# Keys of the last 768 tokens by seven block products, and second channel weights converted later

## The chip, the cores and the metric

The kernel runs on one core of a Trainium2 chip. The metric is the device time of one execution in microseconds; the median of three runs of the kernel before is 672.54 (672.38 to 672.57). TensorE does the matrix products, VectorE (DVE) and ScalarE (ACT) the elementwise work, GpSimd (POOL) some memsets, and SyncE (SP) issues every DMA.

## The reference

Three layers follow each other: windowed attention over 4 batches of 576 tokens and 8 heads of 64, a channel-mixing layer, and a mixer over tokens and channels. Cut to what the change touches:

```python
xk = mu_k * x + (1.0 - mu_k) * x_prev        # x: (4, 576, 512)
k = np.maximum(xk @ w_k, 0.0)                # w_k: (512, 1024)
v = k * k @ w_v                              # w_v: (1024, 512)
r = 1.0 / (1.0 + np.exp(-(xr @ w_r)))
x = r * v
...
h = np.maximum(xt @ w_tok1, 0.0) @ w_tok2    # over tokens
u = x + h.transpose(0, 2, 1)
h2 = np.maximum(u @ w_ch1, 0.0) @ w_ch2      # w_ch1: (512, 1536), w_ch2: (1536, 512)
return u + h2
```

## The kernel before

Every 32-bit product is made of three matmuls (`mm3`): operands are split into a high and a low half (`split`: a copy that rounds, on ScalarE or VectorE, and a subtraction on VectorE), and high x high, high x low and low x high are summed in a PSUM bank.

The stages in order of time. Attention of batch 0 runs first, beside the loading and conversion of `w_k`, `w_v`, `w_r`. Then a loop over `g` = 0 to 49 walks six chunks of 384 tokens (`c, m = divmod(g, 8)`): `prep` mixes each token with the one ahead of it and splits it, `keys(c, m)` makes 128 of the 1024 key columns for the chunk in one bank (4 blocks of 128 input channels, so 12 matmuls), squares and splits them, `mix` multiplies them with `w_v`, `receptance` does `w_r`. The table `beside` spreads the 27 attention units of batches 1 to 3 over the loop, 9 to a chunk pair. Then follow the token stage (`tokens_in`, `tokens_out`), the channel stage's first pass (`middle(c, j)`, 3 chunks of 768 tokens by 6 blocks of 256 hidden columns, results stored in `part_mid`), and its second pass (`result(c)`).

The token stage and both channel passes use seven block products in place of eight (a Strassen form, names A11, S1, A12, S2, S4, S3, A22): sums of quarters of the weights and of the inputs are made first, and the products are accumulated in banks x, y and z. In `middle`, S2, S3 and A22 go on in the bank of A11, S4 in that of S1; between them the bank is copied out (`aside`) or added to others (`part`).

The quarters of the channel weights have to be converted from the stored 64-bit form, combined, split, and stored in DRAM drawers (`part_w0` to `part_w5` for the first weights, `part_A11`, `part_S1` and so on for the second), from which they are fetched later. `weight_1` runs at `g` in `W1_AT`, `weight_2` three times at `g` in `W2_AT`, and three times after the blocks `W2_LATE` = 4, 8, 12 of `middle`. `slowly` lets the planner put such work up to 20 us later than it is written. One conversion of second weights is two loads of 512 KB, 2 x 3 operations to decode, 4 sums, 7 splits and 7 stores of 256 KB. The fetches of all seven products' second weights stand behind `middle` in the program; their places (`w2_at`) are those of the first weights, which the last chunk's blocks set free one after the other, and, for two thirds into A12, a place that the conversions use for their results (slot x2, number 4).

A planner (`Plan.order`) fixes the order of instructions on each engine ahead of the run, with costs of its own and due times counted back from TensorE's order. Each engine then works through its list in order; a DMA on SP that waits holds up the ones behind it. All the work is recorded at one line of the file (L412), so the tile names tell operations apart.

## Time and profile before

| what | value |
|---|---|
| median of three runs | 672.54 us |
| the profiled execution | 672.25 us, span 670.5 us |
| TensorE busy | 657.9 us, 98% of the span, 4129 matmuls |
| VectorE, ScalarE busy | 542.0 and 363.6 us |
| DMA | 138.05 MB, mean 206 GB/s |

Stages on the clock of the span: attention of batch 0 and the start of chunk 0 up to about 69 us, chunks 0 to 3 with attention up to 257, chunks 4 and 5 up to 345, the token stage up to 402, the channel stage's first pass up to 533, its second pass to the end. The profile's first table gives the busy time of each engine; views by stage follow below. A matmul's duration overlaps with the next one's, so that the time of many in a row is read from the pitch of a row without gaps.

### The profile page before, as it was taken

How to read it: one execution, taken by the hardware profiler on the slowest of the kernel's cores; microseconds unless marked ns; L12 is line 12 of the kernel's file. 1: busy time of each engine (PE TensorE's matmuls, PEld its weight loads, DVE VectorE, ACT ScalarE, POOL GpSimd, SP SyncE). 2: the span in 40 equal slices, each digit the busy share in tenths (PEclk: the TensorE clock that was granted, in tenths of full speed). 3: DMA queues.
4: the chain of work that ended last, by engine and by line, in shares of the span. 5: the costliest groups of instructions: out<-in, count | busy, mean ns of one | idle time of the engine just before them, and what ended most of it. 6: DMA issues, size and time to landing. Idle time of an engine off the chain costs nothing.

```text
span 670.5 us, 11406 instructions
## 1 busy us (share of the span) xinstructions
PE 657.9 (98%) x4129; PEld 608.2 (91%) x4129; DVE 542.0 (81%) x1143; ACT 363.6 (54%) x944; POOL 2.3 (0%) x22
## 2 busy tenths in 40 slices
PE   6999999999999999999999999999999999999997
PEld 6778888899898898888889899999999999999997
DVE  3999997799589589588789779698698659899982
ACT  4989775678567568476656346174284222312310
POOL 0000000000000000000000000000000000000000
PEclk9999999999999999999999999999999999999999
DMA  8989343557637243527952118849688999933211
GB/s 316 386 319 320 118 144 99 179 151 233 188 123 240 84 139 119 172 107 271 304 201 62 66 50 288 326 154 322 231 294 281 358 411 412 390 117 94 71 37 59
DMA packets 60776, 138.05 MB, mean 206 GB/s; under 512 B 5296, under 2 KB 23856, under 8 KB 59696
## 3 DMA queue, kind: packets, MB, share of 16 engines
q1 hardware_dynamic: 60720, 137.33, 58.7%
q8 instruction: 32, 0.52, 0.3%
q14 instruction: 24, 0.20, 0.1%
HBM read 91.70 MB, written 45.61 MB: 205 GB/s over the span
## 4 chain that ended last, share of the span: by engine, by line
PE 82%; DMA 10%; DVE 5%; ACT 2%; issue 1%; SPq 0%; DVEq 0%; ACTq 0%
PE bank L412 82%; DMA x<-w_k 2%; DMA z<-part_mid 2%; DMA outT<-y 1%; DMA at<-part_mid 1%; ACT x L412 1%; DVE z L412 1%; DMA wr<-units 1%; DVE wv L412 1%; DMA wv<-units 1%; DVE x L412 1%; DMA raw<-w_v 1%; DVE at L412 1%; DVE xt L412 1%; ACT xt L412 0%
## 5 line engine op out<-in xcount | busy, mean ns | idle before, releaser
L412 PE MATMUL bank<-z,wk 128*128 128x384 f32 x800 | 176.1, 343 | 0.8 <-DVE z L412 0.5
L412 PEld LDWEIGHTS bank<-z,wk 128*128 128x128 f32 x800 | 140.6, 188 | 8.0 <-ACT z L412 1.3
L412 PE MATMUL bank<-wv,z 128*128 128x512 f32 x432 | 126.1, 403 | 0.0
L412 PEld LDWEIGHTS bank<-wv,z 128*128 128x128 f32 x432 | 77.8, 188 | 12.7
L412 ACT ACTIVATE at<-at 128x96 f32<-128x96 f32 (+2 forms) x178 | 64.6, 365 | 35.4 <-DVE at L412 34.1
L412 DVE TENSOR_TENSOR z<-z,z 128x384 fp32r<-128x384 f32 (+1 forms) x94 | 52.9, 570 | 18.7 <-ACT z L412 17.2
L412 PE MATMUL bank<-wr,z 128*128 128x512 f32 x228 | 62.5, 402 | 1.0 <-DVE z L412 1.0
L412 ACT ACTIVATE z<-z 128x384 fp32r<-128x384 f32 (+1 forms) x112 | 57.6, 523 | 6.9 <-DVE z L412 4.0
L412 PE MATMUL bank<-xt,wk 128*128 128x384 f32 x254 | 54.0, 346 | 0.2
L412 PEld LDWEIGHTS bank<-wr,z 128*128 128x128 f32 x228 | 41.4, 188 | 8.5 <-DVE z L412 1.3
L412 PE MATMUL bank<-xt,x 128*128 128x384 f32 x248 | 48.6, 334 | 0.0
L412 PE MATMUL bank<-z,x 128*128 128x384 f32 x232 | 47.1, 335 | 0.3 <-DVE at L412 0.3
L412 PEld LDWEIGHTS bank<-xt,wk 128*128 128x128 f32 x254 | 44.4, 188 | 1.8 <-issue 0.5
L412 DVE TENSOR_TENSOR at<-bank,at 128x384 f32<-128x384 f32 x64 | 35.2, 551 | 12.4 <-PE bank L412 11.9
L412 ACT ACTIVATE z<-bank 128x384 f32<-128x384 f32 (+1 forms) x52 | 25.0, 484 | 35.7 <-PE bank L412 35.5
L412 PEld LDWEIGHTS bank<-xt,x 128*128 128x128 f32 x248 | 43.5, 188 | 0.0
L412 PEld LDWEIGHTS bank<-z,x 128*128 128x128 f32 x232 | 40.7, 188 | 0.7 <-DVE at L412 0.6
L412 DVE SCALAR_TENSOR_TENSOR z<-xt,cst,z 128x256 f32<-128x256 f32 (+3 forms) x92 | 34.1, 402 | 0.2
L412 ACT ACTIVATE x<-bank 96x512 f32<-96x512 f32 (+1 forms) x45 | 26.3, 589 | 10.2 <-PE bank L412 9.9
L412 ACT ACTIVATE at<-bank 128x384 f32<-128x384 f32 x33 | 15.9, 488 | 27.1 <-PE bank L412 26.4
L412 ACT ACTIVATE z<-xt,cst 128x256 f32<-128x256 f32 (+3 forms) x65 | 25.9, 433 | 6.5 <-DVE z L412 6.1
L412 DVE TENSOR_TENSOR raw<-raw 128x256 f32<-128x256 f32 (+1 forms) x68 | 27.7, 421 | 0.9 <-ACT raw L412 0.6
(190 smaller groups left out, 1191.3 us busy)
## 6 DMA issues: line engine op xcount, KB each, us to landing
part_mid<-at SPq DMA_DIRECT2D x18, 768.0 KB, 4.6
z<-part_mid SPq DMA_DIRECT2D x11, 576.0 KB, 8.7
x<-w_c SPq DMA_DIRECT2D x12, 512.0 KB, 4.5
at<-units SPq DMA_DIRECT2D x14, 416.0 KB, 4.7
unit<-units SPq DMA_DIRECT2D x13, 416.0 KB, 4.8
at<-units SPq DMA_DIRECT2D x21, 256.0 KB, 3.8
part_w<-wv SPq DMA_DIRECT2D x21, 256.0 KB, 3.2
part_w<-x SPq DMA_DIRECT2D x21, 256.0 KB, 4.0
```

The lines of the kernel that those rows point to most:

```text
L412: call(kw["out"], kw["constant"]) if method == "memset" else call(**kw)
```

## The change

The keys of chunks 4 and 5 (the last 768 tokens) are made together, by seven block products. New functions: `weight_ks` makes the four sums of quarters of `w_k` for a pair of key blocks j and j + 4, splits and stores them (`part_k0` to `part_k3`), at `g` in `K_AT` = 9, 12, 16, 19; `fetch_k` loads them; `pair_keys(j)` makes the products for blocks j and j + 4 and both chunks. The loop runs over four chunks only, and the code behind it makes keys, `mixes` and `receptance` of chunks 4 and 5. `prep`'s elementwise part becomes `shift`. All six `weight_2` stand after the blocks 4, 6, 8, 10, 12, 14 of `middle`; the first weights are converted at other `g`, and the attention units end at 58 half steps, where they ended at 68. The tracking of DRAM drawers becomes finer (by 384 columns, in `_cells`). Cut to its core:

```diff
-W1_AT, W2_AT, W2_LATE, SLACK = range(10, 34, 4), range(35, 47, 4), (4, 8, 12), 20.0
+W1_AT, K_AT, W2_LATE, SLACK = (8, 11, 13, 16, 18, 21), (9, 12, 16, 19), (4, 6, 8, 10, 12, 14), 20.0
...
-    for n, (lo, hi) in enumerate(([0, 20], [20, 42], [42, 68])):
+    for n, (lo, hi) in enumerate(([0, 20], [20, 40], [40, 58])):
...
+    def weight_ks(j):
+
+        full, sums = at(("raw", 0, 0), (2, 4, 128)), at(("raw", 0, 1024), (4, 2, 128))
+        for i in range(2):
+            combine(full[:, i], *(f(w) for w in wk[j + 4 * i]), ALU.add)
+        (a11, a12), (a21, a22) = ((full[:, i, :2], full[:, i, 2:]) for i in range(2))
+        combine(sums[:, 0], a21, a22, ALU.add)
+        combine(sums[:, 1], sums[:, 0], a11, ALU.subtract)
+        combine(sums[:, 2], a11, a21, ALU.subtract)
+        combine(sums[:, 3], a12, sums[:, 1], ALU.subtract)
+        for n, i in enumerate((0, 1, 3, 2)):
+            t = fresh.tile(2, 2, 128, dtype=F32R)
+            split(sums[:, i], t[:, 0], t[:, 1])
+            nc.sync.dma_start(out=kept_k[j][:, n], in_=f(t.flat(2)))
...
-    nchunk = len(CHUNKS)
+    nchunk = len(CHUNKS) - 2
...
-        if g in W2_AT:
-            slowly(weight_2, W2_AT.index(g), early)
+        if g in K_AT:
+            slowly(weight_ks, K_AT.index(g))
...
+    split(b11, *xk["A11"])
+    combine(d1, b12, b11, ALU.subtract)
+    split(d1, *xk["S1"])
+    split(b21, *xk["A12"])
+    combine(d2, b22, d1, ALU.subtract)
+    split(d2, *xk["S2"])
+    split(b22, *xk["S4"])
+    combine(d1, b22, b12, ALU.subtract)
+    split(d1, *xk["S3"])
+    combine(d2, b21, d2, ALU.subtract)
+    split(d2, *xk["A22"])
...
+    x_r, y_r, z_r, k_ring = psum(0, 3), psum(1, 4), psum(2), psum(3, 4, 0, 1, 2)
...
+    def pair_keys(j, w):
+        x, y, z = (r.tile(N2) for r in (x_r, y_r, z_r))
...
+        on = dict(first=False, goes_on=True)
+        by(x, "A11")
+        s1 = aside(x)
+        by(y, "S1")
+        s5 = aside(y)
+        by(z, "A12")
+        part(k2[4, j], z, s1)
+        by(x, "S2", **on)
+        s2 = aside(x)
+        by(y, "S4", **on)
+        part(k2[5, j], y, s2)
+        by(x, "S3", **on)
+        part(k2[5, j + 4], x, s5)
+        by(x, "A22", **on)
+        relu(k2[4, j + 4], x)
+        square(k2[4, j + 4])
...
+    ws = {j: fetch_k(j) for j in range(2)}
+    for j in range(4):
+        pair_keys(j, ws[j])
+        if j < 2:
+            ws[j + 2] = fetch_k(j + 2)
+        for n in (2 * j - 1, 2 * j):
+            if 0 <= n < 6:
+                mixes(4, n)
...
             if 6 * c + j in W2_LATE:
-                slowly(weight_2, len(W2_AT) + W2_LATE.index(6 * c + j), late)
+                slowly(weight_2, W2_LATE.index(6 * c + j), late)
```

How the order of instructions moves is shown at three places. In the names, the first number is left out where several slots share a name, and the last counts tiles; `part_S_78` is the drawer of S1, `part_A_77` that of A11, `part_A_79` that of A12, `part_S_82` that of S3, `part_A_83` that of A22, and `part_mid_87` holds the first pass's results of chunk 0.

SP before, around the end of the channel stage's first pass (the last two stores of the last conversion come first):

```order
L412 DMA part_A_83<-x_1_4319 128x512
L412 DMA part_S_82<-at_1_2580 128x512
L412 DMA raw_0_316<-part_u_84 128x768
L412 DMA part_mid_89<-at_2_4110 512x1x384
L412 DMA wk_0_370<-part_A_77 128x2048
L412 DMA wk_0_598<-part_A_77 128x1024
L412 DMA part_mid_89<-at_2_4110 512x1x384
L412 DMA wk_0_598<-part_S_78 128x1024
L412 DMA wk_0_711<-part_S_78 128x2048
L412 DMA z_1_5146<-part_mid_87 128x1152
L412 DMA wk_1_778<-part_A_79 128x2048
L412 DMA x_1_4319<-part_A_79 128x1024
```

And SP now, at the same place, from the last conversion's first store (A11) on:

```order
L421 DMA part_A_77<-at_1_3192 128x512
L421 DMA wk_1_782<-part_A_79 128x2048
L421 DMA z_1_5244<-part_mid_87 128x1152
L421 DMA wk_0_602<-part_A_77 128x1024
L421 DMA part_A_79<-x_1_4313 128x512
L421 DMA part_S_78<-x_1_4313 128x512
L421 DMA part_mid_89<-at_2_4116 512x1x384
L421 DMA z_3_5294<-part_mid_87 128x1152
L421 DMA wk_0_715<-part_S_78 128x2048
L421 DMA z_3_5316<-part_mid_87 128x1152
L421 DMA part_S_80<-y_3_4329 128x512
L421 DMA raw_2_3334<-part_mid_87 128x1152
```

The stores of the last conversion, which stood ahead of all fetches, now stand between them; those of S3, A22 and S4 follow further down, and the fetch of A12's last part (into x_1_4313) behind them.

TensorE now, in the new stage for the keys of the last two chunks (bank_63 and bank_66 are the two x banks, bank_64 a y bank):

```order
L421 MATMUL bank_63<-z_0_475,wv_1_597 128x384 x6
L421 MATMUL bank_66<-unit_1_2782,wk_0_715 128x384
L421 MATMUL bank_66<-unit_1_2805,wk_0_715 128x384
L421 MATMUL bank_66<-unit_1_2782,wk_0_715 128x384 x2
L421 MATMUL bank_66<-unit_1_2805,wk_0_715 128x384
L421 MATMUL bank_63<-x_1_2762,raw_1_2895 128x384
L421 MATMUL bank_63<-x_1_1229,raw_1_2895 128x384
```

The first row is S2 of a pair, the last two are the beginning of its S3; between them stand five matmuls of another pair's A22. These rows are new; before, every key block was one group of 12 matmuls in a bank of its own.

VectorE now, at the end of the channel stage's first pass (bank_68, bank_70 and bank_65 hold S1, A12 and the x sum of the very last block; x_1 rows are low halves of the last conversion):

```order
L421 TENSOR_TENSOR x_1_4313<-raw_2_3334,x_1_4313 128x256
L421 COPY at_2_4067<-bank_68 128x384
L421 TENSOR_TENSOR x_1_4313<-raw_2_3334,x_1_4313 128x256
L421 TENSOR_TENSOR at_2_4116<-bank_70,at_2_4067 128x384
L421 TENSOR_SCALAR at_2_4116<-at_2_4116 128x384
L421 TENSOR_TENSOR at_2_4116<-bank_65,at_2_4067 128x384
L421 TENSOR_SCALAR at_2_4116<-at_2_4116 128x384
L421 TENSOR_TENSOR y_3_4329<-raw_2_3334,y_3_4329 128x256
L421 TENSOR_TENSOR at_2_4116<-bank_68,wr_2_4092 128x384
L421 TENSOR_TENSOR at_1_3192<-raw_2_3334,at_1_3192 128x256
L421 TENSOR_TENSOR wv_2_3601<-z_1_5244,wv_2_3601 128x1152
L421 CAST x_1_4313<-raw_2_3334 128x256
```

```order
L421 TENSOR_TENSOR x_1_4313<-raw_2_3334,x_1_4313 128x256
L421 TENSOR_TENSOR wv_2_3601<-z_3_5294,wv_2_3601 128x1152
L421 TENSOR_TENSOR x_1_4313<-raw_2_3334,x_1_4313 128x256
```

The second piece follows directly on the first: the low halves of A22 and S3 around a subtraction that takes a load from `part_mid_87`. Before, VectorE's queue has none of the conversion's operations here.

## Rows read from the trace of the kernel before

**Rows 1.** The page: busy us of each engine, share of the span, instructions.

```profile
PE 657.9 (98%) x4129; PEld 608.2 (91%) x4129; DVE 542.0 (81%) x1143; ACT 363.6 (54%) x944; POOL 2.3 (0%) x22
```

**Rows 2.** Busy us by stage: stretch, length, engines, clock, DMA share, GB/s.

```profile
0.00:69.00 69.00, 60.71 (x472) 50.21 (x473) 57.33 (x126) 55.50 (x174) 1.08 (x20) 1.00 0.90 328
69.00:257.00 188.00, 188.00 (x1348) 167.05 (x1348) 153.75 (x403) 131.35 (x421) 0.00 (x0) 1.00 0.48 152
257.00:345.00 88.00, 88.00 (x442) 77.32 (x441) 68.01 (x178) 54.96 (x128) 1.18 (x2) 1.00 0.65 219
...
402.00:533.00 131.00, 130.71 (x752) 129.72 (x752) 106.91 (x196) 61.27 (x122) 0.00 (x0) 1.00 0.78 281
533.00:670.50 137.50, 133.51 (x767) 132.44 (x765) 108.60 (x117) 29.69 (x28) 0.00 (x0) 1.00 0.54 202
...
68.00:97.00 29.00, 28.50 (x242) 25.08 (x241) 28.68 (x65) 22.71 (x73) 0.00 (x0) 1.00 0.42 121
```

**Rows 3.** What TensorE waited for: us in total, times, longest.

```profile
PE bank L412 <- DMA at<-cst: 4.9, 1, 4.9
...
PE bank L412 <- DVE at L412: 0.9, 3, 0.5
```

**Rows 4.** Timeline of TensorE, 505 to 580 us: start, us, instructions, idle before.

```profile
524.27 4.32 PE L412 MATMUL bank<-z,x 128*128 128x384 f32 x24
...
534.59 1.33 PE L412 MATMUL bank<-z,x 128*128 128x384 f32 x6 [0.28 <-DVE at L412]
...
541.49 7.96 PE L412 MATMUL bank<-xt,wk 128*128 128x384 f32 x45
```

**Rows 5.** Groups by form: count, busy us, mean ns, idle before and its cause.

```profile
L412 DVE TENSOR_TENSOR x<-raw,x 128x256 fp32r<-128x256 f32 x32 | 13.4, 420 | 0.3
...
L412 DVE SCALAR_TENSOR_TENSOR raw<-x,raw 128x512 uint16<-128x512 uint32 x12 | 9.0, 748 | 0.1
...
L412 DVE TENSOR_TENSOR unit<-wv,unit 128x768 f32<-128x768 f32 x6 | 5.7, 950 | 0.0
...
L412 DVE TENSOR_TENSOR wv<-z,wv 128x1152 f32<-128x1152 f32 x5 | 6.8, 1351 | 0.3 <-DMA z<-part_mid 0.3
...
L412 DVE TENSOR_TENSOR at<-bank,at 128x384 f32<-128x384 f32 x64 | 35.2, 551 | 12.4 <-PE bank L412 11.9
L412 ACT ACTIVATE z<-bank 128x384 f32<-128x384 f32 (+1 forms) x52 | 25.0, 484 | 35.7 <-PE bank L412 35.5
```

**Rows 6.** Issues on SP: start, us, instructions.

```profile
522.58 1.57 SPq L412 DMA_DIRECT2D wk<-part_S  x2
```

**Rows 7.** DMA, 505 to 545 us: KB each, median us to landing.

```profile
z<-part_mid SPq DMA_DIRECT2D x3, 576.0 KB, 7.7
...
wk<-part_S SPq DMA_DIRECT2D x1, 1024.0 KB, 8.0
x<-part_S SPq DMA_DIRECT2D x1, 1024.0 KB, 12.7
...
x<-part_A SPq DMA_DIRECT2D x1, 512.0 KB, 9.0
...
part_S<-x SPq DMA_DIRECT2D x1, 256.0 KB, 3.6
...
part_S<-at SPq DMA_DIRECT2D x1, 256.0 KB, 6.0
```

**Rows 8.** DMA, 452 to 482 us: KB each, median us to landing.

```profile
wr<-w_c SPq DMA_DIRECT2D x4, 512.0 KB, 5.6
...
part_A<-x SPq DMA_DIRECT2D x2, 256.0 KB, 2.1
```

**Rows 9.** Busy us in two stretches of 5 us, columns as in rows 2.

```profile
545.00:550.00 5.00, 5.00 (x31) 5.00 (x30) 5.00 (x5) 2.78 (x3) 0.00 (x0) 1.00 1.04 420
575.00:580.00 5.00, 4.85 (x28) 4.53 (x28) 4.22 (x5) 1.56 (x2) 0.00 (x0) 1.00 1.03 418
```

**Rows 10.** The chain that ended last: start, us, what.

```profile
527.58 5.11 DMA z<-part_mid
```

More of the change, by code (lines that the diff above doesn't have):

```diff
@@ L194, in _cells @@
         if not isinstance(a, View):
-            return [a.name]
+            if not a.name.startswith("part"):
+                return [a.name]
+            (row, _), *free = a.ap
+            lo = a.offset % row
+            hi = lo + sum((n - 1) * step for step, n in free)
+            return [(a.name, cell) for cell in range(lo // N2, hi // N2 + 1)]
         offset, ((_, parts), *free) = a.pattern
@@ L682, in prep, with shift @@
         tmp = tmp_r.tile(n)
+        shift(tmp, c, which, kt)
+        r = sets[(c + 1 + which) % 2]
+        h, l = (r.tile(n, dtype=F32R) for _ in range(2))
+        split(tmp, h, l)
+        xs[c, which, kt] = (h, l)
+    def shift(tmp, c, which, kt):
+        pieces = CHUNKS[c]
         col = slice(4 * which + kt, 4 * which + kt + 1)
@@ L699, in prep @@
             o += k
-        r = sets[(c + 1 + which) % 2]
-        h, l = (r.tile(n, dtype=F32R) for _ in range(2))
-        split(tmp, h, l)
-        xs[c, which, kt] = (h, l)
     KT = [2, 3, 0, 1]
@@ L823, in tile_model @@
             k_ring, s_ring = psum(3, 4), psum(0)
-        if 2 * g > [42, 68][1] and s_ring:
-            k_ring, s_ring = psum(3, 4, 0, 1, 2), None
         if m == 0 and c < nchunk:
@@ L852, in tile_model, with product, relu @@
             attend(h, s_ring, t_ring, x_ring)
+    def product(out, a, b, first=True, last=True, goes_on=False):
+        for k, ((ah, al), (bh, bl)) in enumerate(zip(a, b)):
+            mm3(out, ah, al, bh, bl, first and k == 0, last and k == len(b) - 1, goes_on)
+    def relu(out, in_):
+        nc.either(
+            ("scalar", "activation", dict(out=out, in_=in_, func=AF.Relu)),
+            ("vector", "tensor_scalar", dict(out=out, in0=in_, scalar1=0.0, scalar2=None, op0=ALU.max)),
+        )
@@ new lines, in pair_keys, with by, aside, part @@
+    def pair_keys(j, w):
+        x, y, z = (r.tile(N2) for r in (x_r, y_r, z_r))
+        k2[4, j], k2[4, j + 4] = lo_r.tile(N2), lo_r.tile(N2)
+        k2[5, j], k2[5, j + 4] = hi_r.tile(N2), hi_r.tile(N2)
+        def by(out, name, **kw):
+            a, b = ([tuple(v[:, k] for v in hl) for k in range(2)] for hl in (w[name], xk[name]))
+            product(out, a, b, **kw)
+        def aside(p):
+            t = aside_r.tile(N2)
+            copy(t, p)
+            return t
+        def part(t, p, more):
+            combine(t, p, more, ALU.add)
+            relu(t, t)
+            square(t)
+        on = dict(first=False, goes_on=True)
[14 more added lines that the diff above has]
+        square(k2[4, j + 4])
@@ new lines, in tile_model, with mixes @@
+    order_m = [0, 4, 1, 5, 2, 6, 3, 7]
+    def mixes(c, n, first=5):
+        m = order_m[n]
+        h, l = (k2_r.tile(N2, dtype=F32R) for _ in range(2))
+        split(k2[c, m], h, l)
+        for j in range(TILES[c]):
+            if n == 0:
+                vp[j] = bank(first + j, (C,))
+            mm3(vp[j], h[:, rows(j)], l[:, rows(j)], *wv[m], n == 0, n == 7)
+            if n == 7:
+                t = x2[FIRST[c] + j]
+                nc.vector.scalar_tensor_tensor(out=t, in0=t, scalar=1.0, in1=vp[j], op0=ALU.add, op1=ALU.mult)
@@ L1019, in tile_model @@
     tokens_out(B - 1)
-    def product(out, a, b, first=True, last=True, goes_on=False):
-        for k, ((ah, al), (bh, bl)) in enumerate(zip(a, b)):
-            mm3(out, ah, al, bh, bl, first and k == 0, last and k == len(b) - 1, goes_on)
     for j in range(3, 6):
```

61 lines of the change are left out of this document (53 added, 8 removed).

## The prediction

> **What bounds the kernel now.** I read the share of each engine first [rows 1]: TensorE is busy 657.9 us, 98% of the span. Then the busy time by stage [rows 2]: before 69 us TensorE has 8.3 us of gaps (it waits there for inputs and for VectorE), from 69 to 345 us it has none, in the channel stage's first pass 0.29 us, and 4.0 us behind 533 us, nearly all of it the tail after the last matmul. The longest wait of TensorE, 4.9 us, is at the very start [rows 3]. So between 69 and 667 us the time is the number of matmuls by their pitch, and an edit is worth the matmuls that it saves, less the waits that it opens. The pitch of a 128x384 matmul is read from an unbroken row [rows 4]: 24 in 4.32 us; the last one's 0.33 us overlaps nothing behind it, so (4.32 - 0.33) / 23 = 0.1735 us.
>
> The profiled execution took 672.25 us (span 670.5, and 1.75 around it); the median of the runs shown is 672.54, 0.29 above. I sum against 672.25 and add the 0.29 at the end.
>
> **The keys' products.** Before, two chunks of 384 tokens need 2 x 8 x 4 x 3 = 192 matmuls for their keys; now 4 pairs x 7 products x 2 x 3 = 168. Nothing else on TensorE changes in number. 24 x 0.1735 = 4.2 us saved, all of it on the path, since TensorE has no gap there [rows 2].
>
> **What stands beside it.** The seven products need sums of weights (four calls) and of inputs. A call has on VectorE 2 sums of 512 columns, at most 0.75 each, and 8 operations of 256 columns at 0.42 [rows 5], so 4.9; its four copies can go to ScalarE. Four calls add 20 us to VectorE in the stretch 69 to 257 us, where it is busy 153.8 of 188 [rows 2]; 174 of 188 leaves 14, and two attention units that come earlier take part of that. The stretch 68 to 97 us shows VectorE busy 28.68 of 29 with TensorE at 28.50 [rows 2], so such a load is survivable. If this cover were gone, each 1% too much would cost 1.9 us. I take 0.3, between 0 and 2.
>
> In the pairs' own stage VectorE was busy 68 of 88 us [rows 2]. Three conversions of second channel weights leave it, some 7 us each: 11 operations of 256 columns at 0.42, two of 512 at 0.75 [rows 5], and two cheaper ones. About 14 come: five sums and three more low halves of 768 columns at 0.95 and 12 additions at 0.55 [rows 5]. So VectorE hides them. But the order is tight. A product that goes on in a bank has to wait until the bank has been read (TensorE's excerpt shows S2 in bank_63, five other matmuls, then S3 in the same bank: 5 x 0.1735 = 0.87 us for a copy of 0.48 on ScalarE or an addition of 0.55 on VectorE [rows 5], and two hand-overs). I count eight such places in the order, where by these durations the reading operation ends less than 0.1 us ahead of the matmul. Each costs between nothing and 0.5 us, the longest single wait of TensorE for such an addition; the mean there was 0.3 (0.9 in 3) [rows 3]. I take 1.5 for all, between 0 and 4.
>
> **The conversions moved into the channel stage's first pass.** Three of six move from the stage 257 to 345 us into 402 to 533 us. Each loads 2 x 512 KB and stores 7 x 256 KB, 2.8 MB, so 8.5 MB more in 131 us: 65 GB/s on top of 281 [rows 2]; the queue ran at 420 where it was full [rows 9]. VectorE's 3 x 7 = 21 us come on top of 106.9 of 131 [rows 2]: 128 at most, less what ScalarE, with 61.3, takes over of other work. On average both fit, VectorE barely: each 1% too much would cost 1.3 us here. I take nothing for it, since 98.9% was borne in 68 to 97 us. The trouble is at the end. Before, the last conversion's stores all stand ahead of the first fetch (SP's first excerpt); S1's fetches are issued from 522.6 [rows 6], and its product starts at 541.5 [rows 4]. Now the last conversion begins at the fifteenth block of eighteen, and SP alternates stores and fetches of the same tensors (its second excerpt). Each fetch waits for a store of the same quarter, and each store for VectorE.
>
> *First chain, S1.* In VectorE's queue the low half of quarter A12 stands just ahead of the addition behind product A12 of the very last block (VectorE's excerpt, the second x_1 row and the bank_70 row); SP issues A12's store, then S1's. From there to the seventh matmul of the sweep S1 (which needs the late part of its weights) TensorE has 18 matmuls of the block, 36 of the sweep A11 and 6: 60 x 0.1735 = 10.4 us. The chain is 0.42 for the low half [rows 5], a 256 KB store and a 1 MB fetch. A store took 3.6 to 6.0 us and a 1 MB fetch 8.0 in this stretch [rows 7]: 0.4 + 4.2 + 8.0 = 12.6, TensorE waits 2.2. With the emptiest queue shown (2.1 for a store, and 5.6 for a load of half that size, [rows 8]) it is 8.1 and no wait; with the fullest (6.0 and 12.7) it would be 8.7. I take 2.2, since the queue ran full behind it already [rows 9].
>
> *Second chain, A12.* The last third of A12's weights goes into a place that the conversion still uses for S3 and A22. VectorE reaches S3's low half only behind a subtraction that waits for a load of 576 KB (the row of wv_2 from z_3), which can be issued when the last block's matmuls have freed its place: 0.4 + 7.7 [rows 7] + 1.35 + 0.42 [rows 5] + 3.6 + 9.0 [rows 7] = 22.5 us from the start of sweep A11. TensorE needs it after 36 + 36 + 12 matmuls, 14.6 us: 7.9 late. With the emptiest queue (5.1 for that load [rows 10], 2.1, 5.6) it is 15.0, 0.4 late. Both chains count from the same unhindered course, so the second contains the first. I take 5.0 for both together: nearer the upper end, because the stretch was full before the change and gets more bytes; less than the end, because those latencies were seen behind several queued transfers.
>
> VectorE's waits for late loads were there before, one of them 5.1 us of the chain [rows 10], and cost TensorE 0.28 us [rows 4]; that is taken out. If the loads stay late, the second chunk's would be next, but TensorE has six sweeps until then.
>
> **Sum.** 672.25 - 4.2 + 0.3 + 1.5 + 5.0 - 0.3 = 674.55; with the 0.29, 674.8 us, 0.34% slower. About 0.2%, 1.35 us, is what a measurement of this kernel can tell from no change, so the bounds are 671.2 and 673.9.
>
> **The rivals.**
> 1. *The transfers come in time*: the stores and fetches in the transition see a short queue, as at [rows 8]. For it: the first A11 and S1 fetches are issued ahead of the jam. Against it: a DMA share of 1.03 and 1.04 in the stretches behind it [rows 9]. Time: 672.54 - 4.2 + 0.3 + 1.5 - 0.3 = 669.8, faster. Chance 0.20. The Trainium skill, "DMA: Bandwidth & Descriptors", section "Anatomy of one DMA", fits a transfer (on the software path) by 2.0 us and its bytes at 436 GB/s; by that page the first chain would be an estimated 0.4 + 2.6 + 4.4 = 7.4 us, in time. The 8.0 us of the 1 MB fetch [rows 7] are well above that fit, which knows no queue.
> 2. *The waits equal the gain*: only the first chain delays (2.2), or the second is at its middle with a gapless pair stage. 672.54 - 4.2 + 2.2 + 0.3 + 1.5 - 0.3 = 672.0, up to 673.5. For it: the latencies of single transfers spread over a factor of two. Chance 0.25.
> 3. *The forecast*, both chains late, 674 to 677: chance 0.45.
> 4. *VectorE becomes the bound between 69 and 257 us*: sums for the keys, denser attention and first channel weights together. It decides where VectorE's work passes 188 us; 3% beyond costs 5.6 us, and with the forecast's other terms 680. For it: 98.9% busy in 68 to 97 us [rows 2]. Against it: the mean would be 174 of 188, 93%. Chance 0.10.
>
> **How the numbers follow.** Slower: 3 and 4, 0.55. Same: 0.25. Faster: 0.20. The predicted time is the forecast's, 674.8. The range leaves out about half of rival 1 below and most of rival 4 above: 670.0 to 678.5. The forecast's own range is 673.9 to 677.5, from 4.1 to 8 us in the transition.
>
> **What would show it.** In the changed profile TensorE has 24 matmuls less and, at the change from the channel stage's first pass to its second, waits of 2 us or more for loads of the second weights (the releaser would be a DMA into the places wk and x2), where there was 0.28 us before. If those waits are under 1 us in all, rival 1 is right; if VectorE is over 97% busy and TensorE has gaps between 100 and 250 us, rival 4. Waits of tenths of a microsecond in the pair stage for VectorE and ScalarE, 1 to 2 us in all, would confirm that term. A longer time with none of these would make the whole reading wrong.

## The result, and the profile after

The changed kernel takes 680.09 us (679.34 to 680.5, four runs) against 672.56 for the kernel before: slower by 1.09% (ratio 1.0109, interval 1.0096 to 1.0121). The forecast was 674.8 us with a range of 670.0 to 678.5. The sign was right, the size was not: +7.5 us where +2.3 was forecast. The profiled execution took 679.34 us, its span is 677.5.

TensorE has its 24 matmuls less ([rows 1] against the page of after):

```profile
PE 655.7 (97%) x4105; PEld 603.6 (89%) x4105; DVE 568.2 (84%) x1193; ACT 371.2 (55%) x976; POOL 2.3 (0%) x22
```

By stage (columns as in [rows 2]), VectorE is busier by 17 us between 69 and 257 us, where TensorE now has 1.7 us of gaps. The first pass (402 to 533 us) moves more bytes, and behind it the queue is full up to 600 us; TensorE lacks 6 of 67 us there, and its granted clock has a dip:

```profile
69.00:257.00 188.00, 186.29 (x1351) 164.78 (x1350) 170.71 (x436) 145.92 (x472) 0.00 (x0) 1.00 0.57 182
257.00:345.00 88.00, 86.62 (x415) 74.85 (x414) 66.80 (x162) 37.60 (x85) 1.18 (x2) 1.00 0.47 154
402.00:533.00 131.00, 130.59 (x747) 129.25 (x747) 115.94 (x228) 73.63 (x153) 0.00 (x0) 1.00 0.88 314
533.00:600.00 67.00, 61.05 (x340) 59.70 (x340) 52.03 (x59) 18.54 (x18) 0.00 (x0) 0.97 1.02 395
```

TensorE's waits behind 69 us that were not there before, from its timeline (start, length, instructions, idle before and what ended it), first two in the loop over chunks and one in the pair stage, then four in the transition between the channel stage's passes:

```profile
146.92 0.46 PE L421 MATMUL bank<-at 128*128 128x96 f32 x2 [0.39 <-DVE at L421]
...
162.57 0.70 PE L421 MATMUL bank<-wv,z 128*128 128x512 f32 x2 [1.28 <-ACT raw L421]
```

```profile
318.92 2.35 PE L421 MATMUL bank<-wv,z 128*128 128x512 f32 x9 [1.33 <-DVE x L421]
```

```profile
544.49 8.51 PE L421 MATMUL bank<-xt,wk 128*128 128x384 f32 x40 [2.59 <-DMA wk<-part_S]
...
554.27 1.31 PE L421 MATMUL bank<-wv,x 128*128 128x384 f32 x6 [0.74 <-DMA x<-part_A]
...
579.10 3.36 PE L421 MATMUL bank<-xt,wr 128*128 128x384 f32 x18 [1.84 <-issue]
583.24 3.39 PE L421 MATMUL bank<-xt,wr 128*128 128x384 f32 x18 [0.78 <-DVE y L421]
```

Behind the wait of 2.59 us the granted clock is at half, the lower of its two levels (1.2 GHz), until 547.36 us. Windows of 1 us show it (the clock is the figure behind POOL's share):

```profile
545.00:546.00 1.00, 1.00 (x5) 1.00 (x4) 0.00 (x0) 0.11 (x1) 0.00 (x0) 0.50 1.06 425
...
547.00:548.00 1.00, 1.00 (x7) 1.00 (x6) 0.92 (x1) 0.05 (x1) 0.00 (x0) 0.82 1.07 412
548.00:549.00 1.00, 1.00 (x7) 1.00 (x7) 0.97 (x2) 0.97 (x1) 0.00 (x0) 1.00 1.07 424
```

A matmul of 384 columns has a pitch of 0.32 us there in place of 0.1735. It is read from seven in a row and one alone: (2.44 - 0.52) / 6 = 0.32.

```profile
544.98 2.44 PE L421 MATMUL bank<-xt,wk 128*128 128x384 f32 x7
```

```profile
545.30 0.52 PE L421 MATMUL bank<-xt,wk 128*128 128x384 f32 x1
```

The ten matmuls that start from 544.49 us on take 3.15 us until the eleventh starts, where ten pitches at the full clock are 1.74: that is 1.4 us more.

**The ledger.** To see where time is lost I compare the start of the same matmul, counted from the end, in both traces. The one 1600 from the end (390 us, token stage) starts 0.89 us earlier than before: of the 4.16 us saved, 3.27 are spent by then. The one 760 from the end (534 us) is 0.28 earlier, the one 700 from the end 3.38 later, the one 500 from the end 7.06 later, and so is the last. So the transition costs 7.34 us, the stages ahead of it 3.88, and 7.34 + 3.88 - 4.16 = 7.06.

### The profile page after: what moved, and what is told of

Its sections match the earlier page's. It is cut to its first block, busy times and chain, and to the rows that moved or that the text cites. A ratio compares the mean times of both kernels' runs of the same rounds, so it can differ in the third digit from the quotient of the medians.

```text
span 677.5 us, 11577 instructions
## 1 busy us (share of the span) xinstructions
PE 655.7 (97%) x4105; PEld 603.6 (89%) x4105; DVE 568.2 (84%) x1193; ACT 371.2 (55%) x976; POOL 2.3 (0%) x22
## 4 chain that ended last, share of the span: by engine, by line
PE 73%; DMA 12%; DVE 7%; ACT 5%; issue 2%; SPq 1%; DVEq 0%; ACTq 0%
PE bank L421 73%; DVE z L421 3%; DMA x<-w_k 2%; DMA outT<-z 2%; ACT z L421 2%; DMA xt<-w_t 2%; DMA raw<-part_u 1%; DMA wr<-units 1%; DVE at L421 1%; DMA part_mid<-at 1%; DVE x L421 1%; DMA z<-part_mid 1%; DVE wv L421 1%; DMA part_A<-x 1%; ACT xt L421 1%
## 5 line engine op out<-in xcount | busy, mean ns | idle before, releaser
L421 PE MATMUL bank<-z,wk 128*128 128x384 f32 x644 | 142.3, 345 | 0.4 <-ACT z L421 0.3
L421 PEld LDWEIGHTS bank<-z,wk 128*128 128x128 f32 x644 | 112.6, 188 | 6.1 <-ACT z L421 1.0
L421 ACT ACTIVATE at<-at 128x96 f32<-128x96 f32 (+3 forms) x184 | 67.4, 369 | 35.5 <-DVE at L421 33.9
L421 ACT ACTIVATE z<-z 128x384 fp32r<-128x384 f32 (+1 forms) x89 | 45.7, 522 | 22.6 <-DVE z L421 15.6
L421 PE MATMUL bank<-wr,z 128*128 128x512 f32 x192 | 53.6, 405 | 1.2 <-DVE z L421 1.2
L421 DVE TENSOR_TENSOR z<-z,z 128x384 fp32r<-128x384 f32 (+1 forms) x78 | 44.0, 572 | 5.0 <-DMA z<-part_mid 3.3
L421 PEld LDWEIGHTS bank<-wr,z 128*128 128x128 f32 x192 | 34.3, 189 | 7.6 <-DVE z L421 1.5
L421 PE MATMUL bank<-at 128*128 128x96 f32 (+1 forms) x121 | 22.0, 274 | 5.3 <-DMA at<-cst 5.0
L421 PE MATMUL bank<-cst,at 128*96 128x128 f32 x144 | 26.8, 275 | 0.2 <-DVE at L421 0.2
L421 PE MATMUL bank<-wv,x 128*128 128x384 f32 x132 | 24.9, 335 | 0.7 <-DMA x<-part_A 0.7
```

What stands on the lines that cost most here:

```text
L421: call(kw["out"], kw["constant"]) if method == "memset" else call(**kw)
```

## The experiments

Every run is set beside the kernel before on the same chip (medians 671.9 to 672.7). The executions of one kernel spread by 0.9 to 5.1 us, some of it in a wait near 27 us, which was between nothing and 2.5 us in variants that do not differ there. So I read a variant first by TensorE's waits and by the length of the **transition**: from the matmul 900 from the end to the start of the last one. With it stand the bytes moved in the 150 us behind that matmul (sums over windows of 10 us). Where the transition is long, that window ends before the last output stores: to the end of the execution it is 36.1 MB before, 39.9 in the changed kernel, 36.9 in e1 and 39.3 in e9. e12 and e14 to e18 carry e11's edit too.

| kernel | median us | transition us | MB |
|---|---|---|---|
| before | 672.6 | 156.9 | 35.6 |
| changed | 680.1 | 164.4 | 38.7 |
| e1: after 2, 4, 6, 8, 10, 12 | 678.7 | 162.4 | 35.9 |
| e2: after 3, 5, ..., 13 | 684.4 | 169.2 | 37.6 |
| e3: before, all six late | 679.1 | 164.3 | 38.7 |
| e4: no key sums | 678.8 | 167.4 | 38.7 |
| e5: three in the pair stage | 686.0 | 161.0 | 33.7 |
| e6: bytes without sums | 681.8 | 165.0 | 37.1 |
| e7: sums without bytes | 673.4 | 160.6 | 35.1 |
| e8, e11: first weights later | 682.3, 679.7 | 164.8, 165.4 | 38.7 |
| e9: before + 3.1 MB late | 681.9 | 166.6 | 38.1 |
| e10: before + 3.1 MB early | 671.9 | 156.7 | 35.6 |
| e12: three early, own places | 678.6 | 157.9 | 35.3 |
| e13: last two not fetched | 679.6 | 162.2 | 35.8 |
| e14: key sums on GpSimd | 693.6 | 169.4 | 37.4 |
| e15: one early, five in the pass | 673.3 | 157.4 | 35.4 |
| e16: two early, four in the pass | 674.3 | 157.6 | 35.4 |
| e17: e15, two key calls later | 678.0 | 158.8 | 35.3 |
| e18: e17, output on own queue | 674.3 | 156.5 | 35.5 |

### Is it the conversions, and their place?

My first theory was the forecast's: the last conversion stands too late. Then moving all six earlier by one or two blocks cures it (e1, e2), and the kernel before must show the same cost when only its table is changed (e3). Of the changed line only the tables are shown:

```diff
-W2_LATE = (4, 6, 8, 10, 12, 14)
+W2_LATE = (2, 4, 6, 8, 10, 12)     # e1
+W2_LATE = (3, 5, 7, 9, 11, 13)     # e2
```

> The changed kernel with one table moved: the six conversions of second channel weights stand after the blocks 2, 4, 6, 8, 10 and 12 of the channel stage's first pass, in place of 4 to 14. The same bytes and operations, two blocks (about 14.6 us) earlier. Theory A (the last conversion's stores reach into the fetches): TensorE's four waits behind 540 us (2.59, 0.74, 1.84, 0.78 us) and the stretch at a granted clock of 0.5 behind the first of them all but go, under 1 us of them is left, so 680.1 - 7 = about 673 us. Theory B (8.5 MB more in this pass are the cause, wherever they stand): the queue stays full up to the transition, half or more of the waits is left, 676 us or more.

> The same, but after the blocks 3, 5, 7, 9, 11 and 13: one block (7.3 us) earlier than in the changed kernel. Theory A: the first chain was late by 2.6 us and the second by about as much in all, so one block is enough for TensorE's first two waits; the queue is a few transfers shorter, and the waits for VectorE at 578 and 583 us (1.84 and 0.78) should shrink or go: 673 to 675 us. Theory B: 677 us or more, between the changed kernel and the run with 2 to 12 at best.

```diff
-W2_AT, W2_LATE = range(35, 47, 4), (4, 8, 12)
+W2_AT, W2_LATE = (), (4, 6, 8, 10, 12, 14)     # e3, in the kernel before
```

> The kernel before with nothing changed but the table: all six conversions after the blocks 4, 6, 8, 10, 12 and 14 of the first pass, none earlier; keys as before. Theory A: the transition costs the same 7 us as in the changed kernel, 672.5 + 7 = 679.5 us, with TensorE's waits behind 540 us for a second-weight fetch, then a stretch at half the granted clock. Rival C (the pair products' own loads or order are part of the cause of the late transfers): it stays under 675 us.

e3 came out as expected, 679.1 us: the six conversions in the pass cost 7 us without any change to the keys (its transition: 164.3). But e1 and e2 refute the theory that one or two blocks are enough. In e1 the waits at 544 and 554 us are gone, and in their place stands one of 4.08 us later on; e2 is even slower than the changed kernel, with 7.57 us at the same matmul. TensorE's timeline of e1:

```profile
576.46 8.62 PE L421 MATMUL bank<-xt,wr 128*128 128x384 f32 x36 [4.08 <-issue]
```

The profile names nothing as the releaser. On VectorE one sees why TensorE waits: the addition that frees the bank stands behind another that waits for an output store, since the output tiles have three places and the new sum may not be written before the old one has left:

```profile
568.23 1.36 DVE L421 TENSOR_TENSOR xt<-z,xt 128x1152 fp32r<-128x1152 f32 x1
572.68 0.56 DVE L421 TENSOR_TENSOR z<-bank,z 128x384 f32<-128x384 f32 x1 [3.09 <-DMA outT<-z]
573.15 1.35 DVE L421 TENSOR_TENSOR xt<-z,xt 128x1152 fp32r<-128x1152 f32 x1
574.53 1.36 DVE L421 TENSOR_TENSOR z<-z,z 128x1152 f32<-128x1152 f32 x1
575.81 0.55 DVE L421 TENSOR_TENSOR z<-bank,z 128x384 f32<-128x384 f32 x1
```

### Bytes or VectorE's time?

e6 and e7 take the three added conversions apart: one keeps their transfers, the other their arithmetic.

```diff
+    def bytes_2(j, places):              # e6, for the conversions after 6, 10, 14
+        for i in range(2):
+            nc.sync.dma_start(out=places[0].tile(1024, dtype=U32), in_=words(w_c2)[rows(j + 6 * i), :])
+        for name in NAMES:
+            t = places[1].tile(2, 256)
+            nc.gpsimd.memset(out=t, constant=1.0)
+            nc.sync.dma_start(out=kept_w[name][:, j], in_=t)
...                                      # (e6 also sets when the planner places these 14 transfers)
+    def sums_2(j, places):               # e7, for the same
+        for i in range(2):
+            flat = places[0].tile(1024, dtype=U32)
+            nc.gpsimd.memset(out=f(flat), constant=1.0)
+            decode(flat, at(("raw", 0, 512 * i), (512,)))
+        for _ in sums_of((0, 2, 1, 3), places[1]):
+            pass
...                                      # (e7 stores other data into the drawers ahead of the token stage)
```

> The changed kernel, but the three conversions after blocks 6, 10 and 14 keep their two loads of 512 KB and their seven stores of 256 KB and lose all arithmetic on VectorE and ScalarE (the stores hold constants, so a half of the second weights is wrong). Theory B1 (the transfers are what the pass has no room for): TensorE still waits 4 us or more behind 540 us, 676 us or more. Theory B2 (VectorE is full, so the last stores come late): with 21 us less on VectorE the waits go, about 673 us.

> The complement: the conversions after blocks 6, 10 and 14 keep their arithmetic on VectorE and ScalarE and lose their loads and stores; their 21 stores of 256 KB (of other data, so a half of the second weights is wrong) stand ahead of the token stage. Theory B1: the waits behind 540 us go, about 673 us. Theory B2: they stay, 676 us or more. If both halves alone stay above 676 either is enough; if both come out near 673 only the two together are too much.

Without arithmetic it stays slow (681.8), without the bytes it is at 673.4 us. So the transfers it is. The windows from 402 to 510 us of e6, then of e7 (columns as in [rows 2]) show the exchange: 90.5 against 99.2 us of VectorE, 323 against 264 GB/s:

```profile
402.00:510.00 108.00, 107.49 (x616) 106.13 (x615) 90.52 (x165) 53.18 (x107) 7.76 (x14) 1.00 0.90 323
```

```profile
402.00:510.00 108.00, 107.70 (x619) 106.72 (x620) 99.21 (x194) 65.64 (x137) 5.83 (x6) 1.00 0.74 264
```

(e7's profiled execution was the slowest of ten, 675.95 us, and still has a wait of 2.17 us in the transition; the median lies 2.6 us lower.)

### What is a late byte worth, and an early one?

The bytes in the table suggest a new theory: from 510 us on the transfers are the bound, and the kernel before has no slack left in them. The direct test adds 3.1 MB to the kernel before, and nothing else:

```diff
+            if 6 * c + j == 14:          # e9 (e10: == 5)
...
+                for n in range(12):
+                    nc.sync.dma_start(out=spare_d[n], in_=units[n][:, :512])
...                                      # (the planner's times: e9 515 to 545 us, e10 around 445)
```

> The kernel before with twelve copies of 256 KB added (from an input in DRAM to spare drawers that nobody reads), issued between 515 and 545 us, among the first fetches of second weights; no engine but SP has more to do, and no place is touched. 3.1 MB is what the changed kernel moves more than the kernel before after the last third of the first pass (38.7 against 35.6 MB behind the matmul that stands 900 from the end). Theory H (from there to some 585 us the transfers are the bound, and the kernel before has no slack in them: each byte more is paid, at about 410 GB/s): 3.1 MB / 410 GB/s = 7.6 us, 672.4 + 5 to 8 = 677 to 680 us. Theory I (only the place of the last conversion in VectorE's and SP's order counts): under 674 us.

> The same twelve copies, but issued around 445 us, in the first third of the first pass, where the kernel before has its queue busy by half. Theory H: nothing is paid, 672.4 to 673 us. Theory J (the whole pass is short of transfers, so that bytes anywhere in it come back at its end): 675 us or more.

Late they cost 9.5 us, early nothing (ratio 0.9995, interval 0.9981 to 1.0008). 3.1 MB at 410 GB/s is 7.6 us. Of the rest the clock takes 1.6: behind the long wait it is at half for 3.4 us, in which eleven matmuls start where twenty would. TensorE's wait in e9, and VectorE's ahead of it, are those of e1, at the same place:

```profile
581.04 8.06 PE L412 MATMUL bank<-xt,wr 128*128 128x384 f32 x36 [7.55 <-issue]
```

```profile
577.26 0.56 DVE L412 TENSOR_TENSOR z<-bank,z 128x384 f32<-128x384 f32 x1 [6.58 <-DMA outT<-z]
```

e13 takes 3.1 MB out of the changed kernel's transition, behind its first two waits:

```diff
+        if n > 4:
+            w2[name] = w2["S4"]
+            continue
```

> The changed kernel without the fetches of the second weights of S3 and A22 (six loads of 512 KB, 3.1 MB; S4's weights are used in their place, so a part of the output is wrong). They are issued around 558 us, behind the transfers that TensorE's waits at 544 and 554 us are for. If the waits at 579 and 583 us are the same shortage of transfers carried on: these two go (2.6 us) and the first two stay, 680.1 - 2.6 = 677.5 us. If they come from VectorE's order there: all four stay, 680 us.

The waits at 579 and 583 us are gone (one of 0.55 is left), those at 547 to 557 us stay (2.87, 0.92, 0.67), and the transition is 2.2 us shorter. The median, 679.6 of runs between 675.6 and 680.7, shows little of it: its profiled execution lost 2.48 us near 27 us.

### The waits ahead of the transition

e4 leaves out the sums of `w_k` and their splits, with all transfers kept:

```diff
-        combine(full[:, i], *(f(w) for w in wk[j + 4 * i]), ALU.add)
...
-            split(sums[:, i], t[:, 0], t[:, 1])
+        for n in range(4):
+            nc.sync.dma_start(out=kept_k[j][:, n], in_=f(wk2[j][0][:, :2]))
```

> The changed kernel without the sums of w_k: weight_ks stores the high halves of w_k themselves, four stores of 256 KB as before, so all transfers stay and some 10 operations of VectorE and 4 of ScalarE for each of the four calls are left out (the keys of the last 768 tokens are wrong by that). Theory D (VectorE's load of about 20 us between 69 and 257 us makes the waits of 0.39 and 1.28 us at 147 and 162 us): both go, 680.1 - 1.7 = 678.4 us, TensorE without a gap there. Rival E (they come from the denser attention units and first-weight conversions): they stay within a few tenths, 680 us.

Both waits at 147 and 163 us are gone. In the changed kernel VectorE's queue shows half of the second call of `weight_ks` (158.33 to 161.7 us) just ahead of the addition that TensorE waits for (the profile names `raw` of ScalarE, which ended 0.09 us after that addition; it belongs to the decoding of first channel weights, and the matmul neither reads nor writes `raw`):

```profile
158.33 0.68 DVE L421 TENSOR_TENSOR raw<-wk 128x512 f32<-128x512 f32 x1
158.93 0.55 DVE L421 TENSOR_REDUCE at<-at 128x4 f32<-128x384 f32 x1
159.39 1.09 DVE L421 TENSOR_TENSOR raw<-raw 128x256 f32<-128x256 f32 x3
160.61 0.42 DVE L421 TENSOR_TENSOR wv<-raw,wv 128x256 fp32r<-128x256 f32 x1
160.96 0.42 DVE L421 TENSOR_TENSOR raw<-raw 128x256 f32<-128x256 f32 x1
161.40 0.42 DVE L421 TENSOR_TENSOR x<-raw,x 128x256 fp32r<-128x256 f32 x1
161.74 0.68 DVE L421 SCALAR_TENSOR_TENSOR x<-x,bank 128x512 f32<-128x512 f32 x1
```

e17 moves two calls, but the third and fourth, so both waits stay (0.40, 1.26), and the weights of the last pair come late (a wait of 1.43 us at 281 us for `part_k`):

```diff
-K_AT = (9, 12, 16, 19)
+K_AT = (9, 12, 19, 24)     # e17, on e15
```

> The run with one conversion early and five in the first pass (673.3 us), with the third and fourth call of weight_ks at g = 19 and 24 in place of 16 and 19. VectorE was busy 9.84 of 10 us in 160 to 170 us, where a conversion of first weights and the third call stand together, and 8.3, 7.4, 8.1 and 8.4 of 10 in 170 to 190 and 230 to 250 us. If the wait of 1.28 us at 163 us is VectorE's queue there: it goes, 673.3 - 1.3 = 672.0 us. If it is the accumulation's own order: it stays, 673.3 us.

I had named the wrong call. e14 puts the sums on GpSimd:

```diff
-            combine(full[:, i], *(f(w) for w in wk[j + 4 * i]), ALU.add)
+            nc.gpsimd.tensor_tensor(out=full[:, i], in0=f(wk[j + 4 * i][0]), in1=f(wk[j + 4 * i][1]), op=ALU.add)
...                                      # (the four other sums likewise)
```

> The run with the first weights fetched after the token weights (679.7 us), but with the six additions and subtractions of each call of weight_ks on GpSimd in place of VectorE (24 in all, two of 512 columns and four of 256 each); splits and stores as before. If VectorE's time is the cause of the waits at 147 and 163 us, TensorE's waits of 0.4 and 1.3 us there shrink by half or more: 678.5 us. If GpSimd slows VectorE's operations beside it, or its sums come too late, the waits stay or grow: 680 us or more.

It is the slowest of all, 693.6 us. The wait at 163 us is gone, the one at 147 us stays (0.40), eight of 0.27 to 1.92 us come between 172 and 281 us, and the transition, with one wait of 9.06 us, is 4 us longer than e11's. VectorE has 20 instructions less between 69 and 257 us, but is busy for 170.15 us against 170.71, because some of its other operations take longer: a subtraction with two inputs from SBUF does, one with one input from a PSUM bank does not. First the changed kernel's rows, then e14's (mean ns behind the total), and GpSimd's own:

```profile
L421 DVE TENSOR_TENSOR z<-z,z 128x384 fp32r<-128x384 f32 x51 | 27.6, 550 | 0.8 <-ACT z L421 0.3
...
L421 DVE TENSOR_TENSOR at<-bank,at 128x384 f32<-128x384 f32 x22 | 12.1, 550 | 3.5 <-PE bank L421 3.5
```

```profile
L421 DVE TENSOR_TENSOR z<-z,z 128x384 fp32r<-128x384 f32 x51 | 31.5, 628 | 1.2 <-ACT z L421 0.6
...
L421 DVE TENSOR_TENSOR at<-bank,at 128x384 f32<-128x384 f32 x22 | 12.1, 550 | 2.9 <-PE bank L421 2.9
```

```profile
L421 POOL TENSOR_TENSOR raw<-raw 128x256 f32<-128x256 f32 x16 | 13.7, 873 | 0.7
L421 POOL TENSOR_TENSOR raw<-wk 128x512 f32<-128x512 f32 x8 | 11.3, 1414 | 182.0 <-ACT x L421 69.1 <-ACT xt L421 33.6 <-DVE wv L421 30.8
```

The wait at 319 us I had predicted as a matter of bank hand-overs. The trace shows another: VectorE stands 4.3 us at a token weight whose load is queued among fetches of first weights, and the addition stands behind it. VectorE's rows, then ScalarE's, which hands it on:

```profile
311.58 0.56 DVE L421 TENSOR_TENSOR z<-z,z 128x384 fp32r<-128x384 f32 x1
316.46 0.29 DVE L421 TENSOR_SCALAR xt<-xt 128x256 uint32<-128x256 uint32 x1 [4.32 <-ACT xt L421]
...
318.19 1.28 DVE L421 SCALAR_TENSOR_TENSOR x<-x,bank 128x512 f32<-128x512 f32 x2
```

```profile
315.99 0.43 ACT L421 ACTIVATE xt<-xt 128x256 f32<-128x256 f32 x1 [5.82 <-DMA xt<-w_t]
```

```diff
+    start = len(nc.ops)
     for j in range(3):
         fetch_1(j)
+    nc.hold.update(dict.fromkeys(range(start, len(nc.ops)), -25.0))     # e8; 0.0 in e11
```

> The changed kernel with the fetches of the first three blocks of first channel weights (5.5 MB) held back until some 25 us ahead of the token stage. Theory F (the wait of 1.33 us at 319 us is a head-of-line wait: VectorE stands 4.3 us at a token weight whose load of 256 KB is queued behind these fetches, and the addition that frees TensorE's bank stands behind it): the wait goes, 680.1 - 1.3 = 678.8 us, with VectorE's idle time ahead of that load under 1 us. Theory G (as predicted: tight hand-overs of the banks): it stays, 680 us.

> The changed kernel with the fetches of the first three blocks of first channel weights held back until behind the loads of the token weights (some 330 us). Theory F (VectorE's wait for a token weight's load makes TensorE's wait at 319 us; with a fetch queued ahead of those loads VectorE's idle time was 4.3 us and TensorE's wait 1.3, with more of them ahead 6.9 and 2.7): VectorE's idle time falls under 2 us and TensorE's wait goes, 680.1 - 1.3 = 678.8 us. Theory G (tight hand-overs of the banks): the wait stays.

e8 missed its aim: the fetches came just ahead of the last token weights, VectorE's wait grew to 6.9 us and TensorE's to 2.69. That is the same mechanism with more of the cause. In e11 the fetches stand behind, VectorE waits 0.8 us for that load and TensorE not at all there (two waits of 0.28 us come at 346 us). So the wait was a transfer again, not a bank.

### Is there a version that keeps the gain?

With no late bytes the keys' products should pay. e5 puts three conversions behind the pair products, e12 the same with buffers of their own, e15 one and e16 two, the rest early in the pass. Shown are the buffers and the first call of e12, e15 and e16:

```diff
+    early = ring(("wk", 2, 0), ("wk", 2, 1024)), ring(("wk", 1, 1024), ("wk", 1, 1536)), ("wk", 3)
+    slowly(weight_2, 0, early)
     receptance(4, 0, k_ring)
...
-W2_LATE = (4, 6, 8, 10, 12, 14)
+W2_LATE = (4, 8, 12)          # e12 (three early)
+W2_LATE = (2, 4, 6, 9, 12)    # e15 (one early)
+W2_LATE = (2, 5, 8, 12)       # e16 (two early)
```

> The changed kernel with three of the six conversions taken out of the channel stage's first pass and put behind the pair products (beside the mixes and receptances of chunks 4 and 5, in places of the first weights that are free there); the other three after blocks 4, 8 and 12 as in the kernel before. Theory B (the first pass has no room for six conversions, in bytes or on VectorE, wherever in it they stand): the 7 us of the transition go, and what the conversions cost in their new stage comes on top: 680.1 - 7 + 0 to 2 = 673 to 675 us. If something else of the change made the transition late (the finer tracking of drawers, the other order of the fetches), 678 us or more.

> The same, and three of the six conversions behind the pair products, with buffers of their own in the places of the first weights (in the run with three in the pair stage they shared the scratch place raw with the token weights, which came 8 us late); the other three after blocks 4, 8 and 12. Theory H: the transition has no more bytes than in the kernel before and costs at most 4 us more (0.84 and 1.92 us of waits in that run); the wait of 8 us at 367 us goes. 672.5 - 4.2 + 2.2 (ahead of 257 us) + 0 to 4 = 670.5 to 674.5 us. If VectorE is too full between 300 and 400 us, where three conversions of 7 us come on top of 79 of 102, TensorE waits there and it is 676 us or more.

> The changed kernel with the first weights fetched after the token weights, one conversion of second weights behind the pair products (buffers of its own) and five after the blocks 2, 4, 6, 9 and 12 of the first pass. The last conversion stands where that of the kernel before stands, and what is added stands early in the pass. If only late bytes are paid: transition within 1 to 3 us of the kernel before, 672.4 - 4.2 + 2.2 + 1 to 3 = 671.5 to 673.5 us. If five are too many for VectorE (107 + 14 of 131 us), so that the last stores slip: 676 us or more, as with all six after 2 to 12 (678.7).

> The same with two conversions behind the pair products and four after the blocks 2, 5, 8 and 12. One conversion less than in the run with three early (678.6 us, of which 3.1 us were a first-weight fetch that waited for the third conversion's buffers): 672.4 - 4.2 + 2.2 + 0 to 2 = 670.5 to 672.5 us. If the early ones cost TensorE a wait in the stage of the token weights again: 674 us or more.

e12, e15 and e16 bring the transition back to within 1.1 us of the kernel before, at about the same bytes. But the early conversions collide with what stands there: e5 waits 7.97 us at 367 us, since it shares `raw` with the token weights, and e12 waits 3.10 us at 415 us for first weights whose place the conversions held. e16 (674.3) waits 1.53 us at 343 us. e15 is the best of this series, 673.3 us (ratio 1.0011, interval 1.0001 to 1.0021): level with the kernel before, not faster. It still has the waits at 147 and 163 us and one of 1.30 at 577 us.

e18 takes up the output stores, which hold VectorE in the transition, on the order of e17:

```diff
-                nc.sync.dma_start(out=outT[rows(kt + a), at_t:at_t + N2], in_=t)
+                nc.scalar.dma_start(out=outT[rows(kt + a), at_t:at_t + N2], in_=t)
```

> The same, and the output's stores are issued by ScalarE, so on a queue of their own, in place of SP's. In the transition VectorE waits 1 to 3 us ahead of an addition until the store of the tile that it overwrites has left (three places), and TensorE 1.3 us at 576 us for that addition. If the store waits behind the loads in the queue: the wait goes, 672.0 - 1.3 = 670.7 us, 0.25% below the kernel before. If the engines that move the data are full whatever the queue: within 0.3 us of the run with SP's queue.

Against e17 its median is 3.7 us lower (674.3), of which the profiled executions show 2.4 in the transition, now as short as in the kernel before (156.5). VectorE's wait of 2.80 us for an output store is gone, and so is TensorE's of 2.01, whose row in e17 was

```profile
580.75 3.39 PE L421 MATMUL bank<-xt,wr 128*128 128x384 f32 x18 [2.01 <-DVE y L421]
```

The store that VectorE waited for in e17 landed 9.5 us after its issue, the one in its place in e18 after 1.9 (KB each, median us; first e17 at 570 us, then e18 at 569 us):

```profile
outT<-y SPq DMA_DIRECT2D x1, 192.0 KB, 9.5
```

```profile
outT<-y ACTq DMA_DIRECT2D x1, 192.0 KB, 1.9
```

But this is not a store that passes a backlog: in e18 hardly anything moved at that time. From 569 to 570.5 us, first e17, then e18 (the last two figures are the DMA share and GB/s):

```profile
569.00:570.50 1.50, 1.50 (x10) 1.50 (x10) 1.47 (x4) 0.85 (x1) 0.00 (x0) 1.00 1.02 418
```

```profile
569.00:570.50 1.50, 1.50 (x10) 1.50 (x9) 1.47 (x4) 0.33 (x1) 0.00 (x0) 1.00 0.05 19
```

SP issued no load between 560.8 and 570.15 us, as it waited for an output store on the other queue (its waits of 555 to 575 us in e18):

```profile
SPq L421 <- DMA outT<-z: 9.0, 1, 9.0
```

The two stores ahead of it met a full queue in both runs, and landed after 7.8 and 7.7 us in e18, 7.6 and 7.7 in e17. So e18 shows that TensorE's wait goes when this store is in time, not that a queue of its own brings it there.

The Trainium skill, "DMA: Bandwidth & Descriptors", says two things on this: in "Issuing engines are not separate DMA queues", that issuing from several engines saves only the issuing time, and in "Queues, rings and completion order", that each engine that moves data takes turns between the queues it has work for. The trace agrees with the first for those two stores (7.8 and 7.7 us against 7.6 and 7.7). Two later ones landed sooner than in e17 (5.6 and 3.6 us against 8.4 and 6.4), but some 6 to 8 us after the pause, so no run here shows what the turns of the second are worth in a full queue. The output's queue with e15's order, which might beat both kernels, was not run.

## Why the prediction failed, step by step

- **The matmuls**: 24 less, as predicted; the gain of 4.2 us is there at the start of the chain.
- **69 to 257 us**: predicted 0.3 (range 0 to 2), measured 1.7 of waits (some 0.2 us more are lost ahead of 69 us). The mean load was estimated well (174 of 188 us, measured 170.7), and rival 4 is refuted: VectorE is 91% busy, not 97. What was mis-sized is the bunching: the slack of 20 us lets half a call fall onto one place in VectorE's queue, and 9% of room in the mean does not help an addition that stands behind 3.4 us of other work.
- **The pair stage**: predicted 1.5 us in eight small hand-overs, measured 1.33 in one wait. The size fits by luck, the mechanism is wrong: none of the eight shows as a wait of 0.2 us or more, and the one wait is a late load (e8, e11). I looked only at the order of banks there, and not at which loads VectorE's queue passes.
- **First chain (S1)**: predicted 2.2 us, measured 2.59. Of its parts, the store took 6.0 us (predicted 4.2: it is issued at 532.10 and SP's fetch leaves at 538.12) and the fetch 6.4 at most (8.0), as TensorE begins at 544.49. What was missed is what such a wait can do to the clock: 1.4 us more.
- **Second chain (A12)**: predicted 5.0 us for both chains, measured 2.59 + 1.4 + 0.74 = 4.7. Up to here the forecast holds in size, with the clock in place of a part of the second wait.
- **The second chunk**: the step that failed. The text says that the second chunk's loads "would be next, but TensorE has six sweeps until then", and counted nothing. Measured: 1.84 + 0.78 us. TensorE indeed takes up the second chunk at 586.48 us without a wait; it stands earlier, at both halves of A22, the first chunk's last product (`bank<-xt,wr`). VectorE comes to the second chunk's loads before TensorE does, and works through its list in order. The subtraction that prepares the second chunk waits 3.26 us for its load, and the addition that frees the bank for A22 stands behind it. The addition for A22's other half (582.64 us) stands behind one that waits for an output store:

```profile
577.17 1.36 DVE L421 TENSOR_TENSOR z<-z,z 128x1152 f32<-128x1152 f32 x1 [3.26 <-DMA z<-part_mid]
578.45 0.55 DVE L421 TENSOR_TENSOR z<-bank,z 128x384 f32<-128x384 f32 x1
...
580.90 0.56 DVE L421 TENSOR_TENSOR z<-bank,z 128x384 f32<-128x384 f32 x1 [1.23 <-DMA outT<-z]
...
582.64 0.55 DVE L421 TENSOR_TENSOR y<-bank,z 128x384 f32<-128x384 f32 x1
```

In the kernel before, the same subtraction waits for nothing, but the addition behind it ends at 572.58 us and A22 starts at 572.69. So there was 0.1 us of room and not six sweeps:

```profile
570.75 1.36 DVE L412 TENSOR_TENSOR z<-z,z 128x1152 f32<-128x1152 f32 x1
572.03 0.55 DVE L412 TENSOR_TENSOR z<-bank,z 128x384 f32<-128x384 f32 x1
```

The loads are late because the queue is full all the way; in e13, with 3.1 MB less ahead of them, the wait for that load is gone. By [rows 9] the queue already ran at a share of 1.03 and at 418 GB/s at 575 to 580 us in the kernel before. I had read that row, and priced two latencies where a volume was to be priced. By volume the sum would have been: 3.1 MB later than before, / 410 GB/s = 7.6 us, against 7.34 measured. That it comes so near is in part luck: counted to the end of the execution 3.7 MB are late, 9.1 us, and e9 paid 9.5 for 3.1 MB. e9 and e10 show that late bytes cost and early ones do not, e6 and e7 that it is the bytes and not VectorE.

- **The first pass**: predicted 0, measured 0.6 us in small pieces.
- **The last 0.46 us** lie between the profiled execution and the median (0.75 where 0.29 was counted).

Together: 1.5 us more ahead of 390 us, 0.6 in the first pass, 2.6 in the transition (7.34 where 5.0 - 0.3 was counted), 0.46 in the offset; 674.8 + 5.2 = 680.0. (The forecast's own upper end, 8 us in the transition, adds up to 677.8 and not 677.5; nothing hangs on it.) Of the signs that the prediction named, the waits for second weights came (2.59 and 0.74 us, released by DMAs into wk and x2), those of tenths in the pair stage did not.

**What stays open.** The bytes do not explain every transition. Against the changed kernel with 38.7 MB, e2 has 37.6 and takes 4.8 us longer, e14 has 37.4 and takes 5.0 longer, and e4 has as many and takes 3.0 longer. Against the kernel before, e5 has fewer and takes 4 us longer, and e1 has 0.4 MB more, 0.9 us at 410 GB/s, and takes 5.6 longer. For e1 the trace shows a part: at the start of the full stretch its queue moved less than that of the kernel before, and the 1.4 MB that are missing there (3.4 us) come later. First before, then e1:

```profile
510.00:520.00 10.00, 10.00 (x60) 10.00 (x59) 8.16 (x15) 3.10 (x5) 0.00 (x0) 1.00 1.04 350
```

```profile
510.00:520.00 10.00, 10.00 (x59) 10.00 (x59) 8.71 (x17) 6.42 (x12) 0.00 (x0) 1.00 0.67 212
```

No run tests this. In e1, e2 and e5, VectorE's long wait is for an output store (3.1, 5.2 and 2.7 us), so the order in which stores and loads enter the queue counts beside their volume; how much of each wait is the one or the other was not separated.

## What to carry to other kernels

Where a queue is full over a long stretch, price what is moved into that stretch by its volume over the measured rate too, and not only by the latency of the chain that is late first: here 3.1 MB cost 9.5 us in such a stretch, and nothing ahead of it. Ask not only when TensorE needs a late load, but which engine passes it first in its queue, and what stands behind it there. Look in such a stretch for small stores that free a buffer of an engine on the path: in e9 VectorE stood 6.58 us behind one. And a wait that is blamed on one engine's order should be checked for a load at the head of that engine's queue.

## What was not expected of the hardware

The sums on GpSimd made VectorE's subtraction of 384 columns 14% longer in the mean (550 to 628 ns), so that nothing was gained by taking 20 instructions away. The Trainium skill, "SBUF — State Buffer", section "SBUF: two separate sides", describes a pair of ports that VectorE's operations with two inputs from SBUF and GpSimd hold in turn; the trace agrees with it, as VectorE's operation with one input from a bank stayed at 550 ns. The granted clock fell to half in a wait of 2.59 us, and the pitch at the lower level was 0.32 us, 1.85 times that of the full one. Such a wait need not do it: in e13 one of 2.87 us at 547 us left the granted clock at 1.00.
